# Two pairs of token tiles at the start, V before Q and K, transposed blocks in three tiles, dense products in the first cycle

## The chip, the core and the metric

The kernel runs on one core of one Trainium2 chip. The metric is device time in microseconds (us). A core has a matrix engine (PE), a vector engine (DVE), a scalar engine (ACT), a general engine (POOL) and a queue engine (SP) that issues most DMA transfers. Each engine works through its own instructions strictly in the order in which they were built; between engines there are only semaphore waits. An instruction that waits therefore holds up all that stand behind it on its engine.

## The reference

```
xn  = layernorm(x)                                  # x: 2048 tokens x 512
q, k, v = split(xn @ wqkv)                          # 32 heads of 16
att = softmax(q k^T / 4) v  @ wo
z   = gelu(xn @ w_in);  z1, z2 = halves of z        # 896 each
mlp = (z1 * (w_sp @ layernorm(z2) + b_sp)) @ w_out  # w_sp: 2048 x 2048
out = x + att + mlp
```

All in float32.

## The kernel before

Tokens are 16 tiles of 128, in four groups of 512. Every float32 operand of a dense product is split into a high part (rounded to the matrix engine's format) and a low part (the rest), and a product is three matmuls of 512 columns into one accumulator: high by high, low by high, high by low (`mm3`, lines 162 to 164). An activation is split by `split`: ACT writes the high part, DVE subtracts it (lines 157 to 159). A weight is split in two steps, `begin` (load) and `end` (split). In the main part `end` uses POOL for both parts (lines 187 and 188) and tells a planner's estimate of POOL's time, `pool`, that they take 0.6 and 1.3. For the first weights (`early`) the high part is loaded by POOL's own DMA queue, which rounds on the way, and DVE does the subtraction (lines 179 and 185).

There are three phases.

Start-up, lines 797 to 835. `load_x` loads the four tiles of a group in two transfers of 512 KB. `norm_x` is a generator: DVE's statistics of the tiles (lines 244 and 245), a stop, the square root on ACT and two small DVE steps (247 to 249), ACT's normalisation of two tiles, a stop, then the other two (253). With two parts it does this for two tiles at a time. `turn_x` transposes a group on PE, four tiles for each of four columns of 128 (line 259), and splits each column into the operand `xnT`, which is also stored to memory for later use. It takes a new PSUM tile (`spsum`, two banks, three buffers) for each of the four columns. `qk_group` multiplies the group by the Q and K weights of the first eight heads, 12 matmuls each; ACT and DVE split the results (`qk_split`), and SP stores them. `v_tile` multiplies one token tile by the V weights, 12 matmuls, and ACT evacuates it into `vall`. Q, K and V alternate between two accumulators. The order is: group 0 normalised and transposed, Q and K of group 0, V of its first two tiles, group 1 transposed, V of its other tiles, Q and K of group 1, and so on. The generator of a group's normalisation is advanced once for each V tile (line 829), so its parts stand between the V tiles of the group ahead.

Lead-in, 18 half cycles. Row maxima of the scores are found (`max_mm` on PE, `max_red` on DVE, one or two steps in a half cycle) and between them, one group for each half cycle, the dense products of a queue are done: first Q and K of the other heads, `qk_rest`. A product whose weights the planner does not hold ready gives its turn away. The planner's clock counts 2.7 for each half cycle.

Main loop. A cycle of two half cycles does three steps of scores (`scores`), of exponentials on ACT, of products with V (`pv`), and three steps of maxima for later. Dense products fill in for a credit that is refilled once each cycle in proportion to the work left, so that it is used up evenly until cycle 931; in the lead-in (`b < 0`) the credit is a fixed 2600 in every half cycle. The two halves of the first cycle have `b == 0`.

Of the kernel before, what the change touches and what calls it, by code (L numbers as in the profile page):

```python
# [8 lines left out]
F32 = mybir.dt.float32  # L9
# [30 lines left out]
def fused_block(ctx, tc, x, wqkv, wo, w_in, w_spT, b_sp, w_out, out):  # L40
# [59 lines left out]
    def move(dst, src):  # L100
        nc.sync.dma_start(raw(dst), raw(src))
# [38 lines left out]
    def piece(nm):  # L140
        return big.tile([P, 2, 512], F32R, tag="big", name=nm, bufs=RING)
# [11 lines left out]
    def spsum(nm):  # L153

        return ps.tile([P, 2, 512], F32, tag="s", name=nm, bufs=3)
# [12 lines left out]
    def begin(nm, src, n, blocks=1, t=None, early=None):  # L168


        t = piece(nm) if t is None else t
        rw = t512(nm + "r") if early == "t" else big.tile([P, 512], F32, tag="raw", name=nm + "r", bufs=3)
        dst, hi = rw[:, :n], t[:, 0, :n]
        if blocks > 1:
            src = src.rearrange("(c p) f -> p c f", p=P)
            dst, hi = (v.rearrange("p (c f) -> p c f", c=blocks) for v in (dst, hi))
        move(dst, src)
        if early:
            nc.gpsimd.dma_start(hi, src)
        return t, rw, n  # L180

    def end(loaded, early=False):
        t, rw, n = loaded
        if early:
            nc.vector.tensor_sub(t[:, 1, :n], rw[:, :n], t[:, 0, :n].bitcast(F32))
        else:
            gps(0.6).tensor_copy(t[:, 0, :n], rw[:, :n])  # L187
            gps(1.3).tensor_sub(t[:, 1, :n], rw[:, :n], t[:, 0, :n].bitcast(F32))
        return t
# [33 lines left out]
    def load_x(g):  # L223
        xt = [at.tile([P, 2, D], F32, tag="pf", name=f"x{g}_{i}", bufs=PF) for i in (0, 2)]
        for i in range(len(xt)):
            k = 4 // len(xt)
            t = 4 * g + k * i
            rows = x[t * P:(t + k) * P, :]
            move(xt[i], rows if k == 1 else rows.rearrange("(a p) d -> p a d", p=P))
            for j in range(k):  # L230
                xs[g, k * i + j] = xt[i] if k == 1 else xt[i][:, j, :]

    def norm_x(g, parts=1):


        mv = sm.tile([P, 4, 2], F32, tag="mv", name=f"mv{g}", bufs=2)
        rs = sm.tile([P, 2, 4], F32, tag="rs", name=f"rs{g}", bufs=2)
        k = 4 // parts
        for a in range(parts):
            tiles = range(a * k, (a + 1) * k)  # L240
            sl = slice(a * k, (a + 1) * k)
            for i in tiles:
                st = sm.tile([P, 6], F32, tag="bst", name=f"bst{g}_{i}", bufs=4)
                nc.vector.bn_stats(st, xs[g, i])
                nc.vector.bn_aggr(mv[:, i, :], st)
            yield
            nc.scalar.activation(rs[:, 0, sl], mv[:, sl, 1], AF.Sqrt, bias=epst)
            nc.vector.reciprocal(rs[:, 0, sl], rs[:, 0, sl])
            nc.vector.scalar_tensor_tensor(rs[:, 1, sl], mv[:, sl, 0], -1.0, rs[:, 0, sl], ALU.mult, ALU.mult)
            for i in tiles:  # L250
                if i % 4 == 2:
                    yield
                nc.scalar.activation(xs[g, i], xs[g, i], AF.Identity, bias=rs[:, 1, i:i + 1], scale=rs[:, 0, i:i + 1])

    def turn_x(g):
        for c in range(ND):
            pt = spsum(f"xT{g}_{c}")[:, 0, :]
            for i in range(4):
                nc.tensor.transpose(pt[:, i * P:(i + 1) * P], xs[g, i][:, c * P:(c + 1) * P], ident)
            t = piece(f"xnT{g}_{c}")  # L260
            split(t[:, 0, :], t[:, 1, :], pt, 512)
            store(xscr[g][c], t)
            xnT[g, c] = t

    def fetch_xnT(g, k=0):

# [517 lines left out]
    def run(gen):  # L784
        for _ in gen:
            pass
# [7 lines left out]

    engines = {mybir.EngineType.PE, mybir.EngineType.Activation, mybir.EngineType.DVE, mybir.EngineType.Pool, mybir.EngineType.SP}
    with tc.manual_schedule(engines=engines):
        load_x(0)
        w0 = [begin(*qk_weights(0, a), early="t") for a in range(2)]
        load_x(1)
        ones = big.tile([P, 512], F32, tag="raw", name="ones", bufs=3)  # L800
        nc.vector.memset(ones[0:32, 0:P], 1.0)
        wv = []
        for c in range(ND):
            t = (qst, kst)[c // 2][1].rearrange("p (b a f) -> p b a f", b=2, a=2)[:, c % 2]
            wv.append(begin(f"wv{c}", wqkv[c * P:(c + 1) * P, 2 * D:3 * D], 512, t=t, early="rt"[c % 2]))
        nc.gpsimd.dma_start(cscr.rearrange("o (a b) -> (o a) b", b=P), ones[0:16, 0:P])
# [117 lines left out]
        for half in range(-2 * LEAD // 3, 2 * (N // 3 + 4)):  # L924
# [109 lines left out]
```

## Time and profile before

| | us |
|---|---|
| runs before, median of 3 | 1972.23 (1970.47 to 1972.95) |
| the profiled execution | 1971.95 |
| its span | 1970.2 |
| DMA read and written | 294.20 MB, mean 149 GB/s |

In the profile, PEld is the loading of the matrix engine's stationary operand, which overlaps PE. A row of the timeline has the start, the time taken, the engine, the line, the operation, what it writes and reads, the shape and how many instructions are merged in it; in brackets stands the idle time of the engine ahead of it and what ended it. The end of a matmul is modelled and overlaps the next, so the distance of starts is the time that it takes from PE. A row of the page's groups has the line, the count, the busy time, the mean duration in ns and the idle time ahead of the group. Line numbers are those of the kernel before.

### The profile page before, as it was taken

What the parts mean: (1) busy time and instruction counts of PE and PEld (TensorE: products, weight loads), DVE (VectorE), ACT (ScalarE), POOL (GpSimd) and SP (SyncE); (2) the same over time, 40 slices, a digit from 0 to 9 for tenths busy, and PEclk for the clock granted to TensorE, in tenths of its full rate; (3) what the DMA queues carried; (4) which work ended last, traced back from release to release, by engine and by line L of the source; (5) the groups of instructions that cost most, each with busy time, mean ns of one, the idle gap of its engine ahead of it and who ended that gap; (6) DMA issues with size and microseconds to landing.
All of it is one profiled execution on the core that took longest, in us unless ns stands there. A gap on an engine that the chain in (4) does not pass through costs nothing.

```text
span 1970.2 us, 32511 instructions
## 1 busy us (share of the span) xinstructions
PE 1938.4 (98%) x12544; PEld 1046.9 (53%) x12544; DVE 1412.2 (72%) x1628; ACT 1245.2 (63%) x1415; POOL 630.8 (32%) x682
## 2 busy tenths in 40 slices
PE   7999999999999999999999999999999999999998
PEld 6765555555555555555555555555555555554543
DVE  5277777778887777777777777777777777777872
ACT  4336788888776766566666566566566555555664
POOL 2202167779454821026122531017112400002100
PEclk9999999999999999999999999999999999999999
DMA  9587344374534735365554745356464635355323
GB/s 319 189 300 231 118 124 116 105 183 123 139 106 141 203 121 138 91 157 176 124 153 153 210 132 133 94 138 191 108 162 147 184 128 137 112 147 151 105 73 113
DMA packets 234195, 294.20 MB, mean 149 GB/s; under 512 B 34536, under 2 KB 134520, under 8 KB 231160
## 3 DMA queue, kind: packets, MB, share of 16 engines
q1 hardware_dynamic: 229816, 282.08, 49.4%
q0 software_dynamic: 4224, 10.04, 1.4%
q8 instruction: 99, 1.62, 0.4%
q14 instruction: 56, 0.46, 0.1%
HBM read 190.09 MB, written 101.97 MB: 148 GB/s over the span
## 4 chain that ended last, share of the span: by engine, by line
PE 91%; DVE 3%; ACT 2%; DMA 2%; issue 1%; POOL 1%; SPq 0%; DVEq 0%; POOLq 0%; ACTq 0%
PE o L858 23%; PE mx L611 15%; PE st L884 15%; PE sp L162 7%; PE sp L164 5%; PE sp L163 5%; PE qk L162 2%; DVE mm L619 2%; PE mo L162 2%; PE z1p L162 1%; PE z2p L162 1%; PE qk L163 1%; PE qk L164 1%; PE mo L164 1%; PE mo L163 1%
## 5 line engine op out<-in xcount | busy, mean ns | idle before, releaser
L619 DVE TENSOR_REDUCE mm<-mx 128x2 f32<-128x1024 f32 x1024 | 1221.8, 1222 | 467.1 <-PE mx L611 463.9
L57 ACT ACTIVATE pf<-st 128x1024 f32<-128x1024 f32 x1024 | 1028.0, 1024 | 610.8 <-PE st L884 581.1
L858 PE MATMUL o<-pf,vall 128*32 128x512 f32 (+1 forms) x5120 | 511.0, 513 | 0.0
L611 PE MATMUL mx<-kst,qst 48*128 48x512 f32 x2048 | 447.3, 434 | 4.7 <-ACT pf L57 2.3
L884 PE MATMUL st<-qst,kst 50*128 50x512 f32 x2048 | 446.4, 432 | 4.6 <-DMA qst<-mscr 2.3
L611 PEld LDWEIGHTS mx<-kst,qst 48*128 48x128 f32 x2048 | 191.9, 185 | 272.2 <-ACT pf L57 177.0
L884 PEld LDWEIGHTS st<-qst,kst 50*128 50x128 f32 x2048 | 193.2, 185 | 169.5 <-issue 82.1
L858 PEld LDWEIGHTS o<-pf,vall 128*32 128x32 f32 x5120 | 131.4, 109 | 232.8 <-issue 210.9
L162 PE MATMUL sp<-wsp,zs 128*128 128x512 f32 x448 | 194.1, 433 | 0.3 <-DVE z1i L530 0.2
L164 PE MATMUL sp<-wsp,zs 128*128 128x512 f32 x448 | 176.1, 393 | 0.0
L163 PE MATMUL sp<-wsp,zs 128*128 128x512 f32 x448 | 175.8, 393 | 0.0
L537 POOL TENSOR_TENSOR z1i<-z1i,hhl 128x512 f32<-128x512 f32 x28 | 36.1, 1288 | 434.8 <-DVE z1i L530 434.7
L162 PEld LDWEIGHTS sp<-wsp,zs 128*128 128x128 f32 x448 | 83.8, 187 | 69.1 <-issue 52.3
L164 PEld LDWEIGHTS sp<-wsp,zs 128*128 128x128 f32 x448 | 84.1, 188 | 19.6
L163 PEld LDWEIGHTS sp<-wsp,zs 128*128 128x128 f32 x448 | 84.4, 188 | 12.2
L187 POOL CAST wo<-wo0r 128x512 fp32r<-128x512 f32 x1 | 0.6, 611 | 187.3 <-PE mx L611 187.3
L672 POOL TENSOR_TENSOR ob<-ob 128x512 f32<-128x512 f32 (+1 forms) x16 | 21.1, 1317 | 103.3 <-DMA ob<-rscr 80.1
L667 POOL TENSOR_TENSOR ob<-ob 128x512 f32<-128x512 f32 (+1 forms) x16 | 20.5, 1284 | 103.8 <-DMA ob<-escr 96.6
L162 PE MATMUL z2p<-w,xt 128*128 128x448 f32 x128 | 51.4, 402 | 0.0
L162 PE MATMUL mo<-wout,hp 128*128 128x512 f32 x112 | 48.5, 433 | 0.6 <-DVE xr L574 0.4
L164 PE MATMUL z2p<-w,xt 128*128 128x448 f32 x128 | 46.9, 366 | 0.0
L163 PE MATMUL z2p<-w,xt 128*128 128x448 f32 x128 | 46.7, 365 | 0.0
(374 smaller groups left out, 1950.1 us busy)
## 6 DMA issues: line engine op xcount, KB each, us to landing
zs<-z2scr SPq DMA_DIRECT2D x112, 512.0 KB
escr<-e SPq DMA_DIRECT2D x60, 256.0 KB
hscr<-hhl SPq DMA_DIRECT2D x28, 512.0 KB
qst<-qscr SPq DMA_DIRECT2D x30, 384.0 KB
kst<-kscr SPq DMA_DIRECT2D x30, 384.0 KB
xscr<-xnT POOLq DMA_DIRECT2D x16, 512.0 KB, 5.8
qscr<-qkhl SPq DMA_DIRECT2D x16, 512.0 KB
kscr<-qkhl SPq DMA_DIRECT2D x16, 512.0 KB
```

Of the source, the lines that this page charges most:

```text
L57: return nc.scalar.activation(out, in_, func, **kw)
L162: nc.tensor.matmul(acc, lh, rh, start=first, stop=False)
L163: nc.tensor.matmul(acc, ll, rh, start=False, stop=False)
L164: nc.tensor.matmul(acc, lh, rl, start=False, stop=last)
L187: gps(0.6).tensor_copy(t[:, 0, :n], rw[:, :n])
L537: gps(1.3).tensor_add(z1, z1, hl[:, 1, :].bitcast(F32))
L611: nc.tensor.matmul(acc[:, j, :], qst[p % 2][rows, tt * P:(tt + 1) * P], kst[p % 2][rows, kc * 512:(kc + 1) * 512], start=True, stop=True)
L619: dve(1024).tensor_reduce(mmax[i // 16][:, :, t, kc], mstep.pop(i), AX.X, ALU.max)
L667: gps(1.3).tensor_add(both[rows, 0, :], both[rows, 0, :], both[rows, 1, :])
L672: gps(1.3).tensor_mul(both[rows, 0, :], both[rows, 0, :], both[rows, 2, :])
L858: nc.tensor.matmul(acc[cols:cols + VW, a:a + w], vpack(kt - 1 + r, 2 * p + j), pf[:, j * 512 + a:j * 512 + a + w], start=(kt == 1 and a == ...
L884: nc.tensor.matmul(st[:, j, :], kst[p % 2][rows, kt * P:(kt + 1) * P], qst[p % 2][rows, c * 512:(c + 1) * 512], start=True, stop=True)
```

## The change

It does five things.

1. The first group's four tiles come in four transfers of 256 KB, with the first V weight between the second and the third; the other V weights come next, then Q and K weights. POOL's DMA queue loads no weights any more. The high part of the first V weight is made by ACT ahead of the first square root, its low part by DVE; the second and third V weights and the Q and K weights are split by POOL, the fourth V weight by ACT and DVE.
2. The first group is normalised and transposed in two pairs of tiles, and its V products come ahead of its Q and K products. The second pair is transposed in the middle of the second V tile.
3. `turn_x` takes three PSUM tiles in turn; the fourth column goes into the second half of the first tile, and all transposes of a block stand ahead of all splits.
4. The second group is transposed between Q and K of the first. The generator of the third group's normalisation is made there, and is first advanced at the second group's V tiles. Those of the fourth group keep their place.
5. In the main loop the credit is set to 2600 also in the half cycles with `b == 0` in which no product with V was done.

The scratch tile `mhalf` is written by a square root at the very front, which loads ACT's table, and then set again.

```diff
-    def end(loaded, early=False):
+    def end(loaded, low=None, high=False):
         t, rw, n = loaded
-        if early:
-            nc.vector.tensor_sub(t[:, 1, :n], rw[:, :n], t[:, 0, :n].bitcast(F32))
+        if high:
+            low.tensor_sub(t[:, 1, :n], rw[:, :n], t[:, 0, :n].bitcast(F32))
+        elif low:
+            nc.scalar.activation(t[:, 0, :n], rw[:, :n], AF.Copy)
+            low.tensor_sub(t[:, 1, :n], rw[:, :n], t[:, 0, :n].bitcast(F32))
         else:
             gps(0.6).tensor_copy(t[:, 0, :n], rw[:, :n])
             gps(1.3).tensor_sub(t[:, 1, :n], rw[:, :n], t[:, 0, :n].bitcast(F32))
...
-    def turn_x(g):
+    def turn_x(g, lo=0, hi=4):
+
+        tiles = [spsum(f"xT{g}_{lo}_{c}") for c in range(3)]
+        sl = slice(lo * P, hi * P)
         for c in range(ND):
-            pt = spsum(f"xT{g}_{c}")[:, 0, :]
-            for i in range(4):
-                nc.tensor.transpose(pt[:, i * P:(i + 1) * P], xs[g, i][:, c * P:(c + 1) * P], ident)
-            t = piece(f"xnT{g}_{c}")
-            split(t[:, 0, :], t[:, 1, :], pt, 512)
-            store(xscr[g][c], t)
-            xnT[g, c] = t
+            for i in range(lo, hi):
+                nc.tensor.transpose(tiles[c % 3][:, c // 3, i * P:(i + 1) * P], xs[g, i][:, c * P:(c + 1) * P], ident)
+        for c in range(ND):
+            if lo == 0:
+                xnT[g, c] = piece(f"xnT{g}_{c}")
+            t = xnT[g, c]
+            split(t[:, 0, sl], t[:, 1, sl], tiles[c % 3][:, c // 3, sl], (hi - lo) * P)
+            if hi == 4:
+                store(xscr[g][c], t)
...
-    def v_tile(t, ws):
+    def v_tile(t, ws, mid=None):
...
         for c in range(ND):
+            if c == 2 and mid:
+                mid(t + 1)
...
-        load_x(0)
-        w0 = [begin(*qk_weights(0, a), early="t") for a in range(2)]
-        load_x(1)
...
+        nc.scalar.activation(mhalf, epst, AF.Sqrt)
+        nc.vector.memset(mhalf, -0.5)
+        first = load_x(0)
+        next(first)
+        next(first)
         wv = []
         for c in range(ND):
...
+            if c == 0:
+                run(first)
+        w0 = [begin(*qk_weights(0, a), early="t") for a in range(2)]
+        run(load_x(1))
+        run(load_x(2))
...
+        norm = norm_x(0, 2)
+        next(norm)
+        nc.scalar.activation(wv[0][0][:, 0, :], wv[0][1], AF.Copy)
+        next(norm)
+        wv[0] = end(wv[0], nc.vector, True)
+        next(norm)
+        wv[1:3] = [end(l) for l in wv[1:3]]
+        turn_x(0, 0, 2)
+        wv[3] = end(wv[3], nc.vector)
...
-        run(norm_x(0, 2))
-        load_x(2)
-        w0 = [end(l, True) for l in w0]
-        turn_x(0)
-        load_x(3)
+        w0 = [end(l) for l in w0]
+        run(norm)
+        v_tile(0, wv)
+        v_tile(1, wv, lambda t: turn_x(0, 2, 4))
+        norm1 = norm_x(1, 2)
+        next(norm1)
+        v_tile(2, wv)
+        next(norm1)
+        next(norm1)
+        v_tile(3, wv)
+        run(norm1)
+        run(load_x(3))
         init_rows(0)
-        wv = [end(l, True) for l in wv]
-        norm = norm_x(1, 2)
+        turned = []
         for g in range(NG):
             for y in qk_group(0, g, w0, ("d", "o")):
-                if y == 0 and g == 0:
-                    next(norm, 0)
+                if y == 0 and g == 0 and 1 not in turned:
+                    turned.append(1)
+                    turn_x(1)
+                    norm = norm_x(2)
...
-            for t in range(4 * g, 4 * g + 4):
+            for t in range(4 * g, 4 * g + 4) if g else ():
                 next(norm, 0)
                 if t % 4 == 2:
                     if g + 1 < NG:
                         turn_x(g + 1)
                     if g + 2 < NG:
                         norm = norm_x(g + 2)
                 v_tile(t, wv)
...
+            before = done
             for make, n in tiles:
                 make(n)
...
-            if b < 0:
+            if b < 0 or b == 0 and done == before:
                 credit = 2600
```

More of the change, by code (lines that the diff above doesn't have):

```diff
@@ L172, in begin @@
         rw = t512(nm + "r") if early == "t" else big.tile([P, 512], F32, tag="raw", name=nm + "r", bufs=3)
-        dst, hi = rw[:, :n], t[:, 0, :n]
+        dst = rw[:, :n]
         if blocks > 1:
             src = src.rearrange("(c p) f -> p c f", p=P)
-            dst, hi = (v.rearrange("p (c f) -> p c f", c=blocks) for v in (dst, hi))
+            dst = dst.rearrange("p (c f) -> p c f", c=blocks)
         move(dst, src)
-        if early:
-            nc.gpsimd.dma_start(hi, src)
         return t, rw, n
-    def end(loaded, early=False):
+    def end(loaded, low=None, high=False):
         t, rw, n = loaded
-        if early:
-            nc.vector.tensor_sub(t[:, 1, :n], rw[:, :n], t[:, 0, :n].bitcast(F32))
+        if high:
[3 more added lines that the diff above has]
+            low.tensor_sub(t[:, 1, :n], rw[:, :n], t[:, 0, :n].bitcast(F32))
         else:
@@ L225, in load_x @@
         for i in range(len(xt)):
-            k = 4 // len(xt)
+            k = 2
             t = 4 * g + k * i
-            rows = x[t * P:(t + k) * P, :]
-            move(xt[i], rows if k == 1 else rows.rearrange("(a p) d -> p a d", p=P))
             for j in range(k):
-                xs[g, k * i + j] = xt[i] if k == 1 else xt[i][:, j, :]
+                xs[g, k * i + j] = xt[i][:, j, :]
+            if g == 0:
+                for j in range(k):
+                    move(xt[i][:, j, :], x[(t + j) * P:(t + j + 1) * P, :])
+                    yield
+            else:
+                move(xt[i], x[t * P:(t + k) * P, :].rearrange("(a p) d -> p a d", p=P))
     def norm_x(g, parts=1):
@@ L240, in norm_x @@
             tiles = range(a * k, (a + 1) * k)
+            if a:
+                yield
             sl = slice(a * k, (a + 1) * k)
@@ L796, in fused_block @@
     with tc.manual_schedule(engines=engines):
-        load_x(0)
-        w0 = [begin(*qk_weights(0, a), early="t") for a in range(2)]
-        load_x(1)
-        ones = big.tile([P, 512], F32, tag="raw", name="ones", bufs=3)
-        nc.vector.memset(ones[0:32, 0:P], 1.0)
+        nc.scalar.activation(mhalf, epst, AF.Sqrt)
[3 more added lines that the diff above has]
+        next(first)
         wv = []
@@ L805, in fused_block @@
             wv.append(begin(f"wv{c}", wqkv[c * P:(c + 1) * P, 2 * D:3 * D], 512, t=t, early="rt"[c % 2]))
+            if c == 0:
[3 more added lines that the diff above has]
+        run(load_x(2))
+        ones = big.tile([P, 512], F32, tag="raw", name="ones", bufs=3)
+        nc.vector.memset(ones[0:32, 0:P], 1.0)
+        norm = norm_x(0, 2)
[7 more added lines that the diff above has]
+        wv[3] = end(wv[3], nc.vector)
         nc.gpsimd.dma_start(cscr.rearrange("o (a b) -> (o a) b", b=P), ones[0:16, 0:P])
```

## The prediction

> **What bounds the kernel now.** I read the page first, then busy time by stage, then the timeline of the first 170 us.
>
> ```profile
> span 1970.2 us, 32511 instructions
> PE 1938.4 (98%) x12544; PEld 1046.9 (53%) x12544; DVE 1412.2 (72%) x1628; ACT 1245.2 (63%) x1415; POOL 630.8 (32%) x682
> ...
> 0.00:85.00 85.00, 73.42 (x336) 60.19 (x337) 33.94 (x78) 36.02 (x61) 20.44 (x39) 1.00 0.80 283
> 85.00:150.00 65.00, 62.24 (x270) 42.36 (x268) 42.34 (x48) 22.23 (x35) 9.41 (x12) 1.00 0.71 250
> 200.00:600.00 400.00, 397.33 (x2633) 214.38 (x2631) 311.62 (x365) 319.17 (x391) 252.16 (x299) 1.00 0.45 128
> 600.00:1950.00 1350.00, 1344.00 (x8905) 699.40 (x8904) 977.06 (x1086) 827.46 (x882) 334.38 (x316) 1.00 0.50 140
> ```
>
> The columns after a stage are its length and the busy time of PE, weight loads, DVE, ACT and POOL. PE sets the end: from 200 to 1950 us it is idle 2.67 + 6.00 us in all. The count of PE's products does not change, so only its idle time can be gained or lost: 11.6 us up to 85 us, 2.8 us in the next stage (the last 20 us are a drain that the change leaves alone). Every edit lies there. A microsecond of PE saved there should arrive at the end whole, because PE has no slack behind it.
>
> **The start.** In the built order PE's first work is now two tiles transposed and V products, where it was four tiles and then Q.
>
> ```profile
> 2.50:5.00 2.50, 0.00 (x0) 0.00 (x0) 0.44 (x1) 0.00 (x0) 2.50 (x5) 1.00 0.97 352
> ...
> 4.56 0.69 DVE L244 BATCH_NORM_STATS2 bst<-x 128x6 f32<-128x512 f32 x1 [3.48 <-DMA x<-in_x]
> 6.30 0.30 ACT L247 ACTIVATE rs<-mv,epst 128x2 f32<-128x2 f32 x1 [4.30 <-DVE mv L245]
> 7.03 1.52 ACT L253 ACTIVATE x<-x,rs 128x512 f32<-128x512 f32 x2 [0.43 <-DVE rs L249]
> 7.94 0.45 PE L259 MATMUL xT<-ident,x 128*128 128x128 f32 x1 [7.94 <-ACT x L253]
> 10.94 2.18 PE L259 MATMUL xT<-ident,x 128*128 128x128 f32 x9 [0.23 <-ACT x L253]
> 11.45 0.60 ACT L57 ACTIVATE xnT<-xT 128x512 fp32r<-128x512 f32 x1 [0.56 <-PE xT L259]
> 12.05 0.69 DVE L185 TENSOR_TENSOR wqk<-wqk_1r,wqk 128x512 fp32r<-128x512 f32 x1 [2.10 <-DMA wqk<-in_wqkv]
> 14.16 0.77 PE L162 MATMUL qk<-xnT,wqk 128*128 128x512 f32 x1
> 16.44 0.63 PE L164 MATMUL qk<-xnT,wqk 128*128 128x512 f32 x1
> 16.87 0.46 PE L162 MATMUL qk<-xnT,wqk 128*128 128x512 f32 x1
> 17.17 0.39 PE L163 MATMUL qk<-xnT,wqk 128*128 128x512 f32 x1
> 17.40 0.40 PE L164 MATMUL qk<-xnT,wqk 128*128 128x512 f32 x1
> ...
> L57 ACT ACTIVATE qkhl<-qr 128x512 fp32r<-128x512 f32 x24 | 15.2, 633 | 11.0 <-DMA qscr<-qkhl 8.0 <-DMA kscr<-qkhl 2.3
> L57 ACT ACTIVATE e<-o 128x256 f32<-128x256 f32 x1 | 0.4, 385 | 2.4 <-PE o L858 2.4
> L911 DVE COPY e<-o 128x256 f32<-128x256 f32 x1 | 0.4, 425 | 0.2 <-ACT e L57 0.2
> ...
> 69.25 0.62 POOL L187 CAST wqk<-wqk_0r 128x512 fp32r<-128x512 f32 x1
> 69.96 1.30 POOL L188 TENSOR_TENSOR wqk<-wqk_0r,wqk 128x512 fp32r<-128x512 f32 x1
> ```
>
> The first product stands at 14.16 because DVE waited until 12.05 for the POOL queue's copy of a weight and held the token splits behind it. All six such copies (256 KB each) go. At 352 GB/s a block of 256 KB takes 0.74 us. The first 512 KB of x landed at 4.56, so both first tiles are there at 4.56 and the first V weight, next on SP's queue, at 5.30. ACT converts it (0.63) before the square root that stands behind it in its queue: 5.93. Root to first normalisation is 7.03 - 6.30 = 0.73, the two take 1.52: 8.18. Seven transposes remain, 0.21 us apart at this clock ((2.18 - 0.48)/8): the last ends near 10.0. Only the first of the four ACT copies waits for PE, so it waits for all of them; half as wide, it takes 0.39 (the 128x256 row). First V product: **10.4, 3.8 us sooner**. The low part (DVE, 0.43) is there when the second product is due.
>
> The other V weights pass SP in order and land from 7.5 to 9.0. POOL needs 0.62 + 1.30 for each of two, so the second is whole near 11.4; its products are due from 13.0 to 13.8, still 0.43 us apart. The fourth, on ACT and DVE, is done near 12.6 and due after 14. Covered by about 2 us; if x and weights came at half the rate, this cover would be gone (third rival). The Q and K weights follow on POOL (3.8 behind two small memsets) until about 17 and are due after 23, behind all four V tiles. The root moved to the front and the memset behind it end before x lands: nothing.
>
> What runs slow first: products are 0.43 us apart until 16.87 and 0.23 after, although the clock column reads 1.00. So the spacing is the reading, not the column. Six slow ones cost 6 x 0.20 = 1.2 us. Starting at 10.4, the slow stretch lasts 2.7 us as before, or at most until as long after PE's first work as before (7.9 to 16.87, so about 16.4, 6 us of products): excess 1.2 to 2.8. I take 2.0, the middle: **0.8 lost**.
>
> **Blocks of transposes and the third one's wait.**
>
> ```profile
> 26.70 0.60 ACT L57 ACTIVATE vall<-v 128x512 f32<-128x512 f32 x1
> 27.20 1.57 ACT L57 ACTIVATE xnT<-xT 128x512 fp32r<-128x512 f32 x3
> ...
> 30.50 0.68 DVE L244 BATCH_NORM_STATS2 bst<-x 128x6 f32<-128x512 f32 x1
> 33.60 0.18 DVE L245 BATCH_NORM_AGGREGATE mv<-bst 128x2 f32<-128x6 f32 x1
> ...
> 39.99 0.39 PE L162 MATMUL v<-qst,xnT 128*128 128x512 f32 x1
> 40.24 0.60 ACT L57 ACTIVATE qkhl<-qk 128x512 fp32r<-128x512 f32 x1 [2.17 <-PE qk L164]
> 40.87 0.69 DVE L309 TENSOR_TENSOR qkhl<-qk,qkhl 128x512 fp32r<-128x512 f32 x1 [2.08 <-ACT qkhl L57]
> 45.43 1.47 PE L259 MATMUL xT<-ident,x 128*128 128x128 f32 x12
> 47.50 0.66 PE L259 MATMUL xT<-ident,x 128*128 128x128 f32 x4 [0.59 <-DVE xnT L159]
> 47.91 0.48 PE L162 MATMUL v<-qst,xnT 128*128 128x512 f32 x1
> ```
>
> A block of 16 costs PE 47.91 - 45.43 = 2.48 us, as the fourth column waits for a buffer. With the fourth in the first tile's second half it is 16 spaced by 0.11 ((1.47 - 0.27)/11, 0.27 being one alone): 1.8 us. The first group's second pair (8 of them, 0.9) now stands among V products, and the second group's block among Q and K (1.8, and about 0.1 for its last normalised tile): 2.8 against the one block of 2.48 there before, **0.3 lost**. Up to the second group's V products this is -3.8 + 0.8 + 0.3 = **-2.7**.
>
> The third block is the edit that speaks against the change. Before, the third group's statistics ran at 30.50 to 33.78, ahead of the second group's Q and K. Now their generator takes its first step after that K product, because the first group has left the loop that advances it, and its last step stands directly ahead of the block. From the second group's first V product (39.99 before) as zero: ACT takes K at 0.25, DVE ends it at 1.57, four statistics last 3.28 (to 4.8), root to normalisation 0.73, two tiles 1.52 (7.1), then ACT evacuates V (0.5 until the next, 26.70 to 27.20), two more tiles 1.52 (9.1); 13 transposes still follow: the next V product at 10.5. Before it was at 47.91 - 39.99 = 7.92. **2.6 lost** (2.0 if DVE and ACT overlap a little more, 3.2 if the spacing stays wide). PE is idle from 5.4 but for four transposes; everything behind it waits. The fourth block's chain keeps its old place: 2.48 to 1.8, **0.7 gained**.
>
> **Before and in the first cycle.** The weights now converted on POOL advance the planner's estimate of POOL by 7.6 us (four of 1.9), so it holds the next Q weights ready a half cycle later: in the built order six score-maximum steps follow each other without a dense product, where four did, and one dense group of 12 slides out of the lead-in into the first half cycle, which the edited credit rule opens for it.
>
> ```profile
> 95.79 0.97 PE L611 MATMUL mx<-kst,qst 48*128 48x512 f32 x6
> 97.64 0.50 PE L611 MATMUL mx<-kst,qst 48*128 48x512 f32 x2 [0.88 <-DVE mm L619]
> 98.07 0.50 PE L162 MATMUL qk<-xnT,wqk 128*128 128x512 f32 x1
> ...
> 98.10 2.35 DVE L619 TENSOR_REDUCE mm<-mx 128x2 f32<-128x1024 f32 x2
> ...
> 101.01 0.73 PE L611 MATMUL mx<-kst,qst 48*128 48x512 f32 x4
> ...
> 150.03 0.50 PE L611 MATMUL mx<-kst,qst 48*128 48x512 f32 x2 [1.08 <-DVE mm L619]
> ```
>
> The two further steps need buffers that DVE frees near 99.3 and 100.45 (the row at 98.10, half and whole), so dense work resumes at 100.9 where it resumed at 98.07; of these 2.8 us, 0.66 are steps that came after the product before (at 101.01), and 0.2 their own wider spacing: 2.0 to 2.2 lost. The moved group covers DVE's lateness at 150.03: 1.08 gained. **1.1 lost**, between 0.5 (part of the run was idle anyway) and 2.2 (nothing gained). Later the same products fall in other cycles, but from the lead-in on in 354 groups as before: nothing.
>
> **Sum.** -2.7 + 2.6 - 0.7 + 1.1 = +0.3 us. The profiled execution took 1971.95 us (span 1970.2 and 1.75 around it), 0.28 below the median of the runs, 1972.23. Forecast: **1972.3 us**, no change that can be told (0.2%, 3.9 us, is about what a measurement of this kernel tells from none). Its own range, with the bounds above, is 1970.0 to 1975.0.
>
> **Rivals.** First, slower: PE falls back to the slow spacing in the third block's wait, where it does four transposes in nearly 4 us. For: the start shows it slow until 16.87, through all the transposes from 7.94 on. Against: gaps of 1 us (97 and 149) leave it fast. Price: 13 transposes at 0.21 for 0.11, 1.3 us, and six slow products, 1.2; if it stays slow as long as at the start (8.9 us), 14 products, 2.9. With this, 1972.3 + 4.2 = 1976.5; it decides from five microseconds of slow products on. [...]
>
> Second, faster: the moved products break up waits in the long part. PE idles 8.7 us from 200 on; half of that gone, 4.3 us, gives 1968.0. For: which dense product meets which evacuation does change. Against: as many groups, and idle time scattered over 1750 us.
>
> Third, the change does not start PE as early as it says: x and weights are on one queue, and if that alone carries half of 352 GB/s, the first V weight lands at 7.5 rather than 5.3 and the start gains 1.6, not 3.8: 1974.5. For: POOL's queue moved bytes beside it. Against: the 352 row has few of those yet.
>
> **How the numbers follow.** Forecast 0.50, all within 0.2%. First rival 0.20, of which 0.13 beyond 1976.2. Second 0.17, faster. Third 0.10, of which 0.03 slower, with a long slow start. The rest, 0.03, is waits not seen, 0.02 of it slower. Together faster 0.17, same 0.65, slower 0.18. The range runs from 1967.5 (second rival) to 1977.0 (first): about one in ten lies outside on either side.
>
> **What would show it.** PE's first V product near 10.4, with no wait for weights; the spacing 0.43 until 13 to 16.5. PE waiting for ACT's x in the third block of transposes for some 3.5 us in four pieces, the next product 10.5 after the second group's first V product, and its spacing there 0.23 (forecast) or 0.43 (first rival). The fourth block at 1.8. Idle near 2.6 us in a run of six maximum steps, and no wait after the first scores. Wrong would be: PE past the third block earlier than before by over 1.5 us, or idle time from 200 us on that differs by over 2 us.

## The result, and the profile after

The changed kernel takes 1980.71 us (median of 6 runs, 1979.03 to 1981.71), the kernel before 1972.59 (6 runs, 1969.27 to 1976.31): ratio 1.0046, 95% interval 1.0035 to 1.0057. It is slower by 8.1 us, outside the predicted range. The profiled execution took 1979.03, with a span 7.1 us longer than before. Places below are compared on the two profiled executions, kernels by the ratios of their runs. Executions of one kernel differ with the clock that PE was granted: of 29 of the kernel before, measured beside the first experiments, the fourteen with a mean granted clock of 0.998 or more took 1968.4 to 1972.3 us, the five with 0.995 took 1975.2 to 1977.6. Line numbers are the changed kernel's (in the experiments they shift by a few lines): products L162 to L164, transposes L268, normalisation L260, maxima L625 and L633, scores L922, products with V L896.

Busy time by stage, the changed kernel (columns as before: length, PE, weight loads, DVE, ACT, POOL, granted clock, DMA share, GB/s):

```profile
0.00:85.00 85.00, 74.57 (x337) 61.41 (x338) 31.62 (x79) 37.42 (x68) 23.97 (x41) 0.98 0.74 265
85.00:150.00 65.00, 62.05 (x257) 42.06 (x255) 40.93 (x46) 20.08 (x32) 9.38 (x12) 0.95 0.66 232
150.00:200.00 50.00, 46.48 (x290) 25.19 (x292) 36.68 (x43) 33.13 (x41) 10.75 (x12) 1.00 0.81 239
200.00:600.00 400.00, 395.69 (x2610) 212.84 (x2606) 306.20 (x357) 317.20 (x388) 249.23 (x300) 1.00 0.45 128
600.00:1950.00 1350.00, 1346.65 (x8909) 701.45 (x8910) 985.84 (x1097) 826.93 (x882) 338.11 (x319) 1.00 0.50 141
```

The one stage of the kernel before that the prediction did not show:

```profile
150.00:200.00 50.00, 49.97 (x319) 26.50 (x320) 40.13 (x46) 35.93 (x44) 14.32 (x16) 1.00 0.79 236
```

Take the idle time of PE from these rows. Up to 1950 us it is 24.6 us after and 23.0 before. The span grew by 7.1, so most of the loss is no idle time at all: PE is busy and slow. The clock column says where, 0.98 and 0.95 in the first two stages, where it was 1.00. The idle time that is new stands from 150 to 200 us: 3.52 where it was 0.03. From 200 us on it is 7.7 instead of 8.7: 1.6 more up to 600 us and 2.7 less behind it.

The timeline of the changed kernel, from the start to the second block of dense work:

```profile
10.33 0.80 PE L162 MATMUL v<-qst,xnT 128*128 128x512 f32 x1 [0.47 <-ACT xnT L57]
...
14.37 0.47 PE L162 MATMUL v<-kst,xnT 128*128 128x512 f32 x1
...
36.89 0.39 PE L162 MATMUL v<-qst,xnT 128*128 128x512 f32 x1
...
43.30 0.33 PE L268 MATMUL xT<-ident,x 128*128 128x128 f32 x1 [0.81 <-ACT x L260]
...
45.19 0.45 PE L268 MATMUL xT<-ident,x 128*128 128x128 f32 x1 [0.85 <-ACT x L260]
45.89 2.97 PE L268 MATMUL xT<-ident,x 128*128 128x128 f32 x13 [0.26 <-ACT x L260]
48.58 0.52 PE L162 MATMUL v<-qst,xnT 128*128 128x512 f32 x1
48.94 0.40 PE L163 MATMUL v<-qst,xnT 128*128 128x512 f32 x1
...
65.05 1.91 PE L268 MATMUL xT<-ident,x 128*128 128x128 f32 x16
66.72 0.47 PE L162 MATMUL v<-qst,xnT 128*128 128x512 f32 x1
...
95.67 0.97 PE L625 MATMUL mx<-kst,qst 48*128 48x512 f32 x6
97.52 0.50 PE L625 MATMUL mx<-kst,qst 48*128 48x512 f32 x2 [0.88 <-DVE mm L633]
99.25 0.49 PE L625 MATMUL mx<-kst,qst 48*128 48x512 f32 x2 [1.23 <-DVE mm L633]
100.38 0.79 PE L625 MATMUL mx<-kst,qst 48*128 48x512 f32 x2 [0.64 <-DVE mm L633]
101.11 0.79 PE L162 MATMUL qk<-xnT,wqk 128*128 128x512 f32 x1
101.70 0.63 PE L163 MATMUL qk<-xnT,wqk 128*128 128x512 f32 x1
...
106.52 0.57 PE L625 MATMUL mx<-kst,qst 48*128 48x512 f32 x2
```

Four places are to be read here. The first product comes 3.8 us sooner (10.33 for 14.16), and the second group's first V product 3.1 (36.89 for 39.99). Behind the third block the next product comes 48.58 - 36.89 = 11.7 us after that, where it was 7.9: the 13 transposes that follow the last normalised tile stand 0.21 us apart ((48.58 - 45.89)/13), half speed, and the products are fast again from 48.94 on. The fourth block takes 1.7 us. Behind the run of six maximum steps dense work resumes at 101.11, but its 12 products take 106.52 - 101.11 = 5.4 us instead of 2.9: they too are at half speed. Windows of the changed kernel on the first slow stretch, on what follows it and on the second:

```profile
45.26:48.67 3.41, 3.15 (x15) 2.86 (x15) 0.00 (x0) 0.58 (x1) 0.00 (x0) 0.50 0.66 209
48.67:52.09 3.42, 3.42 (x17) 2.85 (x16) 2.56 (x5) 2.51 (x5) 1.44 (x3) 1.00 0.40 138
99.87:106.70 6.83, 6.32 (x16) 4.26 (x16) 4.45 (x5) 0.07 (x1) 0.12 (x1) 0.50 0.92 293
```

The granted clock is half for 3.41 us at the third block and for 6.83 us around the end of the run of six. Behind the start these two are the only slow stretches of this execution until the drain at its end; the profiled execution of the kernel before has none.

The first cycle of the kernel before, then of the changed one:

```profile
147.97 0.50 PE L884 MATMUL st<-qst,kst 50*128 50x512 f32 x2
...
153.64 0.64 PE L858 MATMUL o<-pf,vall 128*32 128x512 f32 x4
```

```profile
148.82 0.50 PE L922 MATMUL st<-qst,kst 50*128 50x512 f32 x2
...
149.39 1.94 ACT L57 ACTIVATE pf<-st 128x1024 f32<-128x1024 f32 x2 [0.67 <-PE st L922]
151.21 0.60 ACT L57 ACTIVATE qr<-qk 128x512 f32<-128x512 f32 x1
151.87 0.50 PE L162 MATMUL qk<-xnT__1195,wqk 128*128 128x512 f32 x1 [2.07 <-ACT qr L57]
...
157.17 0.50 PE L162 MATMUL qk<-xnT__1195,wqk 128*128 128x512 f32 x1 [1.37 <-ACT qr L57]
...
161.02 1.07 PE L896 MATMUL o<-pf,vall 128*32 128x512 f32 x8
```

A dense group now waits twice, 2.07 and 1.37 us. In the main loop the dense groups share one accumulator (two only while `now[0] < -2`, line 301). ACT frees it with the copy `qr`, and that copy was built behind the half cycle's exponentials `pf`: it starts at 151.21, when they are done, and PE's next product at 151.87. The first scores are 0.9 us later than before and one group of 12 (2.9 us) has not been done yet: 3.8 behind. At the first product with V it is 7.4 later with 6 more products done (1.4): 6.0 behind. Behind it the difference is not steady. At the same product with V, with as many dense products done in both kernels, it is 6.7 us at 431 us, 9.1 at 618, 9.5 at 1789 and 6.4 at 1817 (times of the kernel before), and 7.1 at the end. Of the 2.4 lost between 431 and 618, the row from 200 to 600 us shows 1.6 as idle time. The 3 given back lie where the kernel before waits 1.49 and 0.80 us for a transfer (`qst<-mscr`, at 1795 and 1797); the changed kernel has no such wait there.

### The profile page after: what moved, and what is told of

Read it like the earlier page. It is cut to its first block, busy times and chain, and to the rows that moved or that the text cites. A ratio compares the mean times of both kernels' runs of the same rounds, so it can differ in the third digit from the quotient of the medians.

```text
span 1977.3 us, 32500 instructions
## 1 busy us (share of the span) xinstructions
PE 1943.5 (98%) x12544; PEld 1050.1 (53%) x12544; DVE 1410.0 (71%) x1629; ACT 1245.2 (63%) x1422; POOL 631.9 (32%) x684
## 4 chain that ended last, share of the span: by engine, by line
PE 90%; DVE 4%; ACT 4%; issue 1%; POOL 1%; DMA 1%; SPq 0%; DVEq 0%; ACTq 0%; POOLq 0%
PE o L896 22%; PE mx L625 15%; PE st L922 14%; PE sp L162 7%; PE sp L164 5%; PE sp L163 5%; DVE mm L633 2%; ACT pf L57 2%; PE qk L162 2%; PE mo L162 2%; PE qk L163 2%; PE qk L164 1%; PE z1p L162 1%; PE mo L163 1%; PE mo L164 1%
## 5 line engine op out<-in xcount | busy, mean ns | idle before, releaser
L633 DVE TENSOR_REDUCE mm<-mx 128x2 f32<-128x1024 f32 x1024 | 1220.8, 1221 | 475.0 <-PE mx L625 472.0
L896 PE MATMUL o<-pf,vall 128*32 128x512 f32 (+1 forms) x5120 | 511.1, 514 | 0.0
L625 PE MATMUL mx<-kst,qst 48*128 48x512 f32 x2048 | 449.1, 436 | 4.7 <-DVE mm L633 2.7
L922 PE MATMUL st<-qst,kst 50*128 50x512 f32 x2048 | 445.9, 432 | 4.2 <-DVE mm L633 3.2
L625 PEld LDWEIGHTS mx<-kst,qst 48*128 48x128 f32 x2048 | 192.2, 185 | 273.7 <-ACT pf L57 175.7
L922 PEld LDWEIGHTS st<-qst,kst 50*128 50x128 f32 x2048 | 192.9, 185 | 169.6 <-issue 82.3
L896 PEld LDWEIGHTS o<-pf,vall 128*32 128x32 f32 x5120 | 131.5, 109 | 232.4 <-issue 210.5
L162 PE MATMUL sp<-wsp,zs 128*128 128x512 f32 x448 | 194.1, 433 | 0.3 <-DVE z1i L544 0.2
L164 PE MATMUL sp<-wsp,zs 128*128 128x512 f32 x448 | 176.0, 393 | 0.0
L162 PEld LDWEIGHTS sp<-wsp,zs 128*128 128x128 f32 x448 | 83.9, 187 | 69.8 <-issue 53.0
L164 PEld LDWEIGHTS sp<-wsp,zs 128*128 128x128 f32 x448 | 84.1, 188 | 19.4
L162 PE MATMUL z2p<-w,xt 128*128 128x448 f32 x128 | 51.5, 402 | 0.0
L162 PE MATMUL mo<-wout,hp 128*128 128x512 f32 x112 | 48.5, 433 | 0.6 <-DVE xr L588 0.4
L355 POOL TENSOR_TENSOR z<-z 128x512 f32<-128x512 f32 x28 | 30.3, 1083 | 52.7 <-ACT z L57 52.7
L686 POOL TENSOR_TENSOR ob<-ob 128x512 f32<-128x512 f32 (+1 forms) x16 | 20.5, 1284 | 82.4 <-DMA ob<-rscr 81.8
L164 PE MATMUL z2p<-w,xt 128*128 128x448 f32 x128 | 46.9, 366 | 0.0
```

The source lines that it names most:

```text
L162: nc.tensor.matmul(acc, lh, rh, start=first, stop=False)
L164: nc.tensor.matmul(acc, lh, rl, start=False, stop=last)
L355: gps(0.0022 * n).tensor_mul(u, x, x)
L625: nc.tensor.matmul(acc[:, j, :], qst[p % 2][rows, tt * P:(tt + 1) * P], kst[p % 2][rows, kc * 512:(kc + 1) * 512], start=True, stop=True)
L633: dve(1024).tensor_reduce(mmax[i // 16][:, :, t, kc], mstep.pop(i), AX.X, ALU.max)
L686: gps(1.3).tensor_mul(both[rows, 0, :], both[rows, 0, :], both[rows, 2, :])
```

## Experiments

**Parts of the change undone.** Four kernels, all edits of the changed one.

```diff
 e1_credit_off                 # the credit rule of before
-            if b < 0 or b == 0 and done == before:
+            if b < 0:
 e2_planner                    # POOL's estimate set back after the start
         turned = []
+        pool[0] = -1000.0
 e3_stats                      # third group's statistics again ahead of the second group's Q and K
             load_stacks(0, slice(g * 512, (g + 1) * 512))
+            if g == 0:
+                next(norm)
 e4_three                      # all three
```

> Theory (in the first cycle each dense group needs the one accumulator that ACT frees only behind the exponentials of that half): the two PE waits for ACT's evacuation of a Q or K product, 2.07 and 1.37 us, are gone, a wait of about 1.1 us for DVE is back at the first cycle, and the kernel takes 2.3 us less than the changed one. Rival (these waits only bring work forward that is saved later): no difference beyond 0.5 us, first product with V earlier but the end the same.

> The planner's estimate of POOL is set back behind the start-up, nothing else. Theory (the estimate alone makes the run of six maximum steps, and PE's idle time in that run makes the next products slow): the run is four steps again with one wait near 0.9, products after it 0.23 apart, 16 dense groups ahead of the first scores; 4.8 us less than the changed kernel (2.1 idle, 2.4 slow products, 0.3 slow steps), of which the first cycle may give back up to 1. Rival (the slow products come from something else in the start-up): products behind the run still 0.43 apart, 2.1 us less.

> The third group's statistics are issued behind the first group's K product. Theory (third block waits for the late chain of statistics, root and normalisation, and its transposes are slow because PE idled): from the second group's first V product to that behind the third block 7.2 us for 11.7, transposes 0.11 apart, at most 0.3 lost where the statistics stand ahead of a Q split; 4.2 us less than the changed kernel. Rival (the lead-in waits for something else, such as POOL's weights or the stores, and takes the gain back): lead-in begins 4 us earlier but the end gains less than 1.

> All three edits. Theory: they add up, 11.3 us less than the changed kernel, 1969.4 us, 3.2 less than the kernel before. Rival (the gains overlap, since the slow clock is shared or the long part gives the time back): no faster than before.

| | us, median | ratio to before | 95% |
|---|---|---|---|
| changed kernel | 1980.71 | 1.0046 | 1.0035 to 1.0057 |
| e1_credit_off | 1978.29 | 1.0030 | 1.0021 to 1.0039 |
| e2_planner | 1978.48 | 1.0028 | 1.0017 to 1.0039 |
| e3_stats | 1974.67 | 1.0015 | 1.0005 to 1.0025 |
| e4_three | 1967.34 | 0.9967 | 0.9954 to 0.9980 |

The credit rule: -2.4 us by the medians and -3.2 by the ratios, where 2.3 were expected; its interval overlaps that of the changed kernel. Its timeline has no wait for `qr`, and the old wait for DVE is back in its place and of its size:

```profile
151.45 0.50 PE L625 MATMUL mx<-kst,qst 48*128 48x512 f32 x2 [1.08 <-DVE mm L633]
```

The statistics: -6.0 by the medians, where 4.2 were expected; the intervals allow both. The third block is whole and fast, as its timeline shows:

```profile
43.90 1.91 PE L268 MATMUL xT<-ident,x 128*128 128x128 f32 x16
```

The planner: -2.2 by the medians and -3.5 by the ratios, where 4.8 were expected. The run is four steps again and the products behind it are fast, but PE slowed down in two other places. Its timeline and, below, its windows there:

```profile
151.67 0.50 PE L162 MATMUL qk<-xnT__1187,wqk 128*128 128x512 f32 x1 [2.07 <-ACT qr L57]
...
153.56 0.63 PE L164 MATMUL qk<-xnT__1189,wqk 128*128 128x512 f32 x1
153.99 0.63 PE L162 MATMUL qk<-xnT__1191,wqk 128*128 128x512 f32 x1
...
447.45 0.50 PE L923 MATMUL st<-qst,kst 50*128 50x512 f32 x2 [0.84 <-DVE mm L633]
448.32 0.50 PE L625 MATMUL mx<-kst,qst 48*128 48x512 f32 x2 [0.36 <-ACT pf L57]
```

```profile
152.00:155.50 3.50, 3.50 (x10) 2.72 (x9) 0.00 (x0) 0.28 (x1) 0.00 (x0) 0.53 1.01 350
448.90:452.40 3.50, 3.50 (x17) 1.02 (x15) 1.96 (x2) 3.47 (x5) 3.33 (x4) 0.54 0.75 206
```

In both stretches of 3.5 us the granted clock is near half (0.53 and 0.54) and PE never idle. The first follows the 2.07 wait, which left the products fast in the changed kernel itself. The second is new: the corrected order of groups together with the credit rule leaves two half cycles near 445 us without a dense group, with 1.2 us of waits and six short steps on end. Eight products 0.2 us late each, 1.4 in the second stretch and its waits of 1.2 make some 4 us, more than what is missing. All three edits together take 13.4 us off by the medians; 11.3 were expected, and the single gains add up to 10.6. With all three neither of the two slow places exists, PE is not idle at all from 150 to 200 us, and the kernel beats the one before:

```profile
150.00:200.00 50.00, 50.00 (x332) 26.19 (x325) 39.97 (x45) 35.24 (x43) 14.32 (x16) 1.00 0.78 230
```

**Parts of the change done alone, on the kernel before.** `x1_turn_only` takes over the new `turn_x` and nothing else, `x2_credit_only` the credit rule (written more shortly: in the lead-in no product with V is done, so `done == before` holds there).

```diff
 x2_credit_only
+            before = done
...
-            if b < 0:
+            if b <= 0 and done == before:
```

> The kernel before with the new transposes alone (three tiles in turn, the fourth column in the first tile's second half); order of start, V tiles, weights, credit as before. Theory (the fourth column waits for a buffer: 2.48 us a block of 16 where 1.8 are needed): the second, third and fourth group's blocks lose 0.68 each, 2.0 in all, and the first product of the start may come up to 0.8 sooner: 1969.5 to 1970.3 beside 1972.3 before. Rival (the blocks wait for ACT's normalised tiles and the copies, not for the buffer; or the copies now all come behind the last transpose): no change, 1972.3, with the block still near 2.5 us.

> The kernel before with the edited credit rule alone: the first cycle's half cycles without a finished key block get dense products too. Theory from the two runs so far (one accumulator is used in that cycle; a dense group waits there until ACT has evacuated the one before it behind two exponentials): two waits of 2.1 and 1.4 us for the accumulator appear and the one of 1.08 for DVE goes: +2.3, 1974.6; another 1.5 if the clock falls after the longer wait, as in the run with the planner held. Rival (the prediction's step: the moved group covers DVE's lateness): -1.1, 1971.2.

x1: 1969.24 beside 1971.42 in the same session, ratio 0.9994 (0.9985 to 1.0004). By time alone that is not told from none (2.0 us less were expected), but its timeline shows each piece:

```profile
14.46 0.79 PE L162 MATMUL qk<-xnT,wqk 128*128 128x512 f32 x1 [0.69 <-ACT xnT L57]
...
27.51 1.94 PE L261 MATMUL xT<-ident,x 128*128 128x128 f32 x16
29.20 0.47 PE L162 MATMUL v<-qst,xnT 128*128 128x512 f32 x1
```

A later block costs 29.20 - 27.51 = 1.69 where it was 2.48: 0.8 gained on each. At the start there is a small price, since all splits stand behind all transposes: PE waits 0.69 for the first, and the first product is 0.3 later than before, not sooner.

x2: 1978.19 beside 1971.42, ratio 1.0037 (1.0023 to 1.0052): 7 us lost by an edit of one line. The two waits are there, 2.07 and 1.38. Behind the first one the products go to half speed, in the timeline of x2:

```profile
150.32 0.50 PE L162 MATMUL qk<-xnT__1176,wqk 128*128 128x512 f32 x1 [2.07 <-ACT qr L57]
...
151.74 0.63 PE L164 MATMUL qk<-xnT__1178,wqk 128*128 128x512 f32 x1
152.16 0.63 PE L162 MATMUL qk<-xnT__1180,wqk 128*128 128x512 f32 x1
```

for 3.4 us (granted clock 0.83 from 150 to 160 us), and again from 448 us, as in the run with the planner set back but for about twice as long (products slow until 454.96, granted clock 0.97 from 400 to 500 us). The granted clock of the whole execution is 0.994, by my estimate some 24 us at half (0.006 x 1979.6 x 2), of which 10 lie at the drain (0.84 from 1950 us on). The two profiled spans differ by 9.4 us; the waits (2.3 more than before) and what the other 14 us at half clock can lose (at most 7) account for most of that. Expected were 3.8 together.

**The accumulator.** `x3_two_acc` gives the changed kernel two accumulators in the first cycle, `y3_credit_two` the same to x2, `y2_best` to the changed kernel with planner and statistics mended and the credit rule kept.

```diff
-            if now[0] < -2 and m:
+            if now[0] < 1 and m:
```

> The changed kernel with two accumulators for dense groups in the first cycle as well, where it has them only ahead of it. Theory (the waits of 2.1 and 1.4 are for the one accumulator): both go and with them nearly 3.4 us, 1977.3. Rival a (the second accumulator is also that of the first PV products, so one wait of 1.4 to 2 moves there): 1978.7 to 1979.3. Rival b (the waits are DVE's or ACT's lateness, whichever product stands there): 1980.7.

> The kernel before with the edited credit rule and two accumulators in the first cycle. Theory (the rule by itself cost 7 us: two waits of 3.4 in all, less 1.08, and half-rate spells of some 1.5 each behind them and near 449 us, where the order of groups it leads to puts six short steps together): without the waits 3.4 and one spell go, the spell near 449 stays: 1971.4 to 1973. Rival a (the prediction's step, true once the accumulator is free): 1970.3. Rival b (the loss was the later order of groups alone): 1977 to 1978, as with one accumulator.

> The changed kernel with the planner's estimate of POOL corrected, the third group's statistics in their old place, and two accumulators in the first cycle; the edited credit rule stays. Theory (each cause acts by itself): beside the run of three edits (ratio 0.9967), which had the credit rule off, the two accumulators with the rule on are worth what they showed against the rule off, 0.002 less 0.003 of ratio, so about 0.9957, 1963.5 beside 1972 before. Rival (with the other waits gone, PE is ahead of DVE and the first cycle gives nothing back): 0.9967, 1965.5.

x3: 1975.56, ratio 1.0020 (1.0011 to 1.0029), 5 us below the changed kernel, where 3.4 were expected. Both waits are gone and nothing took their place; the rest beyond 3.4 is within the intervals. So the accumulator was the cause. y3: 1977.06, 1.0023 (1.0013 to 1.0033), 1971.4 to 1973 expected; y2: 1973.07, 1.0004 (0.9996 to 1.0013), 5.7 above e4_three, which has the credit rule off. Both missed for the same reason. In their order of groups the last dense group of the first cycle takes the accumulator `o`, which the first products with V need (they wait 2.04 us for it in y2 and 2.0 in y3). The timeline of y2:

```profile
155.67 1.06 PE L899 MATMUL o<-pf,vall 128*32 128x512 f32 x8 [2.04 <-ACT qr L57]
...
158.46 0.63 PE L163 MATMUL qk<-xnT__1361,wqk 128*128 128x512 f32 x1
158.88 0.63 PE L164 MATMUL qk<-xnT__1361,wqk 128*128 128x512 f32 x1
```

The wait of 2 us has moved to the products with V, and behind it PE is slow once more (products 0.43 us apart in y2; granted clock 0.97 from 150 to 200 us in both); near 445 us both are slow again, as x2 is (0.94 and 0.97 from 400 to 450 us). So the rule was worth nothing: x2 stands above the same kernel without it, and so do y3 and y2, which have the second accumulator besides; only x3 stands below its pair, e1, by 0.001 of ratio, which the intervals don't tell from none.

**Why PE slows down behind the run of six.** Unused products fill the waits of the changed kernel's run. `x4_fill` puts thirteen of 48 rows between its steps and behind the last, `y1_fill128` nine of 128 rows and `y1_fill48` the same nine with 48 rows. The edit of x4 is like that of y1_fill128, with other counts and other operands of 48 rows.

```diff
 y1_fill128
             for make, n in tiles:
                 make(n)
+                k = {(-15, 1): 3, (-14, 0): 4, (-13, 0): 2}.get((half, tiles.index((make, n))), 0)
+                if k:
+                    acc = ps.tile([P, 512], F32, tag="o", name=f"idle{half}_{n}", bufs=1)
+                    for _ in range(k):
+                        nc.tensor.matmul(acc, wq[1, 0][:, 0, 0:P], wq[1, 0][:, 0, 0:512], start=True, stop=True)
 y1_fill48
-                        nc.tensor.matmul(acc, wq[1, 0][:, 0, 0:P], wq[1, 0][:, 0, 0:512], start=True, stop=True)
+                        nc.tensor.matmul(acc, wq[1, 0][0:KS, 0, 0:P], wq[1, 0][0:KS, 0, 0:512], start=True, stop=True)
```

> The changed kernel with unused products (48 rows by 512, results never read) put between the maximum steps of the run of six in the lead-in, so that PE is busy there while DVE catches up. Theory (the 12 products behind the run are 0.43 us apart because PE was mostly idle for some 4 us before them, and the clock fell): these products are 0.23 apart and the time falls by up to 2.4 us though more is computed, 1978.3. Rival (the slow spacing does not hang on the idle time there, but on where the clock's own period falls): spacing 0.43 as before, 1980.7 to 1981.2.

> The changed kernel with nine unused products (128 rows, 128 columns, 512 wide, results never read) between the maximum steps of the run of six: three, four and two of them. Theory, formed on the run with thirteen unused products of 48 rows, which left PE no idle time there and stayed slow: the clock falls for want of full-size products, since those of 48 rows count for little; with full-size ones the 12 products behind the run are 0.23 apart and the time is up to 2.4 below the changed kernel's, 1978.3. Rival (the clock's period alone, or the sort of work ahead, decides): 0.43 apart, 1980.7.

> The same nine unused products in the same places from the same tile, 48 rows of it instead of 128. Theory (products of 48 rows count for little): 12 products 0.43 apart behind the run, 1980.7. Rival (idle time is what counts, and nine products take enough of it away): 0.23 apart, 1978.3, as with 128 rows.

| | us, median | ratio to before | 95% | spacing behind the run |
|---|---|---|---|---|
| changed kernel | 1980.71 | 1.0046 | 1.0035 to 1.0057 | 0.43 |
| x4_fill | 1980.22 | 1.0047 | 1.0034 to 1.0060 | 0.43 |
| y1_fill48 | 1979.63 | 1.0038 | 1.0025 to 1.0051 | 0.43 |
| y1_fill128 | 1977.38 | 1.0026 | 1.0017 to 1.0034 | 0.23 |

Windows of x4, the run and what follows it:

```profile
97.00:100.30 3.30, 3.13 (x16) 1.87 (x15) 3.30 (x4) 0.71 (x2) 0.00 (x0) 1.00 0.21 81
100.30:107.20 6.90, 6.90 (x20) 4.74 (x18) 4.66 (x5) 0.00 (x0) 0.47 (x1) 0.52 0.99 308
```

Timeline of y1_fill48 behind the run, then of y1_fill128:

```profile
103.38 0.63 PE L163 MATMUL qk<-xnT,wqk 128*128 128x512 f32 x1
103.80 0.63 PE L164 MATMUL qk<-xnT,wqk 128*128 128x512 f32 x1
```

```profile
102.02 0.39 PE L163 MATMUL qk<-xnT,wqk 128*128 128x512 f32 x1
102.25 0.39 PE L164 MATMUL qk<-xnT,wqk 128*128 128x512 f32 x1
```

In x4 PE is busy for 3.13 of 3.30 us ahead of the drop, and the clock still falls to half (0.52 over the 6.90 us behind it). So idle time did not decide there, and my first theory fell. With the same nine products in the same places the number of rows made the difference between the two traces: with 48 the products behind the run are 0.43 us apart, with 128 they are 0.23. Their times differ by 2.2 us in the medians, near the 2.4 expected, though the two intervals overlap. That it is so near is partly luck: in the trace of y1_fill48 only six of the twelve products behind the run are slow (granted clock 0.52 from 102.10 to 105.50, 0.98 from there to 109.00), and PE is slow again in the stage from 150 to 200 us, where the granted clock is 0.97 and that of y1_fill128 1.00. The spacing is that of the first products behind the run, read from one trace for each; of the runs that leave the run of six unfilled, e1 and e3 were slow there too (0.43 apart), and x3 has a granted clock of 0.97 from 85 to 150 us.

## Why the prediction was wrong

**The start, right.** First V product at 10.33 (10.4 said), second group's V 3.1 sooner (2.7 said), slow spacing until 14.37. Half rate on a single queue did not come: ACT took the first V weight at 5.29, where the working put 5.30.

**The third block, right in its chain and short in its spacing.** The statistics, the root, ACT's evacuation of V between the tiles: the last normalised tile was ready for PE 9.0 us after the second group's first V product, where the working put 9.1. The term "13 transposes still follow: the next V product at 10.5" was mis-sized: they took 2.7 us at 0.21 instead of 1.4 at 0.11, so the loss was 3.8, not 2.6. The bound "3.2 if the spacing stays wide" was short too. That was half of the first rival, priced at 1.3 + 1.2; the slow products behind it did not come (fast from 48.94). The granted clock was half from 45.26 to 48.67 (0.50) and full behind it (1.00), and that stretch held the 13 transposes (45.89 to 48.58) and hardly a product, so here the clock came back behind transposes; 16 of them also ran 0.10 us apart in the fourth block (1.67 us), at a granted clock of 1.00.

**The fourth block, right:** 1.7 us for the 1.8 said.

**The lead-in: the step that costs the run of six at "2.0 to 2.2" failed.** Dense work resumed at 101.11 (100.9 said), with PE idle 2.75 us in the run, as worked out. But I took the 12 products behind it at the fast spacing. They were slow and lost 2.4 us more. The prediction did have the mechanism, with a chance of 0.20, and at the third block alone; against it I set "gaps of 1 us leave it fast", which was read where PE went at most 3.0 us without a full-size product (in the kernel before 95.79 to 98.07 and 147.97 to 151.01). In the run of six it went 5.4 us without one (95.67 to 101.11), and the working had not asked for such places.

**The first cycle: "The moved group covers DVE's lateness at 150.03: 1.08 gained" was wrong in sign.** The wait for DVE did go, but 3.4 us of waiting for the accumulator came. The group that fills a gap must have a place to write to, and the place's release was built behind 1.9 us of exponentials on the in-order ACT. The working never asked what the moved products wait for.

**The long part: "nothing" came near by luck.** From the first product with V to 618 us 3.1 more were lost, 1.6 of them as idle time in the row to 600 us; near 1795 3.0 came back with the waits for `qst<-mscr`, and about 1 is lost in sum. The second rival's mechanism, waits broken up, is in those 3.0 if the new order removed them. That is open: e4_three, which has no wait for `qr`, waits 1.2 us for `qst<-mscr`.

Summed on the profiled execution: -3.1 at the start, +3.8, -0.7 and -0.1 for the rest up to the lead-in; +3.9 there (106.52 - 101.01 less 0.66 for the two steps, and 0.1 of lead: 4.9 up to the next step, of which 1 was made up later in the lead-in); +2.2 in the first cycle; +1.1 after it: 7.1. The forecast for these was -2.7, +2.6, -0.7, +2.2, -1.1 and 0.

## What to carry to other kernels

Before you move work into a gap, list what the moved work itself waits for: its buffer is freed by an engine whose queue may have the gap's own long instructions in front of that release (here 1.9 us of exponentials). When you count a stretch with few full-size products, price not only its idle time but also the slower clock of the work behind it (here 2.75 us idle and 2.4 more in 12 slow products), and look for every such stretch, not only the one that the edit names. An estimate that a planner keeps is part of an edit: here 7.6 us booked on POOL at the start changed the order 80 us later.

## What the runs showed of the hardware

PE's granted clock fell to half where PE had been busy for 3.13 of 3.30 us with products of 48 rows (x4: a granted clock of 1.00 there, then 0.52 over 6.90 us). y1_fill48 and y1_fill128 differ in the rows alone: behind the run of six the granted clock is 0.52 from 102.10 to 105.50 us in the first and 1.00 from 102.00 to 109.00 in the second. It fell as well at 449 us in e2 (0.54 from 448.90 to 452.40), with 1.2 us of waits among scores and maxima of 48 and 50 rows and products with V of 32 columns. In the traces of the kernel before and the changed one the granted clock is 1.00 or 0.50 (at the start of the changed kernel it reads 1.00, though the products are 0.43 us apart until 14.37). Between the start and the drain it is half for 3.41 us (from 45.26) and for twice that, 6.83 (from 99.87), in the changed kernel, and these falls and that of its drain (1970.38) stand whole multiples of 3.413 us apart (16 and 548 of them); the kernel before has its only fall at its drain (1962.58). In e2 the products behind the wait of the first cycle are slow for 3.4 us too (152.2 to 155.6). What brings the clock down was not shown beyond this: whether rows, columns or both matter, and from what share on, was not tried.

The same wait of 2.07 us in the first cycle was followed by slow products in x2 and e2 (0.43 us apart) and by fast ones in the changed kernel (0.23). y1_fill48, x4 and y1_fill128 have it too (2.1); from 150 to 200 us the granted clock is 0.97 in x2, e2 and y1_fill48 and 1.00 in the changed kernel, x4 and y1_fill128. Steps of 3.413 us, counted in each trace from a fall of its clock, tell the first three apart. The steps are an estimate from the lengths and distances above; between the falls no trace marks them.

| | wait | step | clock behind it |
|---|---|---|---|
| x2 | 148.25 to 150.32 | 148.0 to 151.4 | half |
| e2 | 149.60 to 151.67 | 148.8 to 152.2 | half |
| changed kernel | 149.80 to 151.87 | ends at 151.07, inside the wait | full |

In x2 and e2, where the wait lies whole in one step, the clock was half from the end of that step; in the changed kernel, where a step's end divides it, it was not. No run set that position, and three traces are few, but if it held, the price of such a wait would change from one execution to the next.
